# Float64 weights rounded inside four staging places, one per token block; the first layer's last output products moved into the second layer

## The chip, the core and the metric

The kernel runs on one core of a Trainium2 chip. The metric is device microseconds of one execution: the median of three runs before the change is 740.58 us (739.4 to 743.11). The profiled execution took 738.42 us, of which 736.6 us is the span from its first to its last instruction.

## The reference

`x` is (4, 8, 512, 64) and `state` (4, 8, 32, 64). A small attention step reads the state for each token and the tokens for each state row; its result, 2304 rows (4 x 512 tokens and 4 x 32 state rows) of 512, goes through two feed-forward layers:

```
h = x @ w_in;  g = max(h,0) + alpha*min(h,0);   x = g @ w_out      # layer 0: 512 -> 2048 -> 512
h = x @ w_in2; g = max(h,0) + log1p(exp(-|h|)); out = g @ w_out2   # layer 1: the same sizes
```

The weights arrive as float64. The kernel gets them as 64-bit integers and rounds them to float32 on the core.

## The kernel before, in words

**Precision.** Every float32 operand of a product is a pair (hi, lo): hi is a rounded copy, lo the rest, and a product is three matmuls, hi*hi, hi*lo, lo*hi (`mm3`, L180; `product`, L567). `split` (L185) makes a pair: a copy on ACT, a subtraction on DVE or POOL.

**Rounding one weight tile.** There are 64 tiles of 128x512, listed in `wsrc` (L193): 32 of layer 0 and 32 of layer 1, kinds `i` (w_in) and `o` (w_out). `wload` (L236) brings one tile's 64-bit words into one of three staging places `stg` (a fourth, borrowed from the accumulators, serves tile 3 alone). Five steps round it: `conv_a` on ACT (two passes, L264 and L265), `conv_j`, `conv_f`, `conv_v` on DVE (L269, L275, L279) and `conv_g` on POOL (L285). The result goes into one of three places `cnv`, taken round-robin by `cslot` (L257), except for layer 0's `i` tiles, which go to their own place. `wprep` (L296) then either splits the tile (layer 0, `o`) or stores it in DRAM (layer 1, L304). A staging place is free after `conv_v`, a `cnv` place after the split or the store has read it. `wo_load` (L481) brings stored `o` tiles back, also through `cnv`, and splits them from there.

**Layer 0** goes over four quarters q of the 2048 hidden columns. The attention step, quarter 0 and the first blocks of quarter 1 are in an order written out by hand (`ORDER`, L48). The rest is the loop at L911: per quarter 16 token blocks (b, fc) and one block of state rows (b = B). One block is `hidden` (6 matmuls), `act` (ACT `Relu` L398, DVE `prelu` L390, then `split` with both halves taken from PSUM) and `out_part` (12 matmuls, taken into the accumulators at L436 after each fourth block); `out_part` runs three blocks behind (`LAG`), from the list `todo`. `wconv` is called once per block, `wprep` as often as `READY` (L74) lists that block.

**Layer 1** is 16 groups (p, n). A group makes seven products (`product`, L571), additions of them on DVE (L474), four activations (three ACT passes L401 to L403, DVE L404, split) and the output products of the group before (`pair_out`, L580, taken in at L593). Its operands are cut and combined on ACT and POOL in `w_steps`, `y_first`, `y_second`. In the groups of p = 0, `wprep` is called three times per group (L987, L993, L1015) for the tiles that are left. Group (0, 0) begins by emptying `todo`: the three output products left from layer 0 (L962).

**Order.** Outside `ORDER` a planner places the instructions on the engines' queues by their order in the program and by its own estimate of when each is ready. On the chip each queue runs in order: an instruction that waits holds everything behind it. Loads, stores and reloads all leave from SP's queue. `psa` and `psb` have four PSUM banks each: `psa` for hidden values and layer 1's products, `psb` for output sums.

Of the kernel before, what the change touches and what calls it, by code (L numbers as in the profile page):

```python
# [8 lines left out]
F32 = mybir.dt.float32  # L9
# [9 lines left out]
P = 128  # L19
# [41 lines left out]
l13 I0 h14 v15 l14 D15 L18 g15 O14 J0 H16 w10 A16 C16 O15 p10 G16 q10 D16 H17 Q15 H18 A17 O16 C17 A18 G17
C18 D17 G18 D18 H19 h15 Q16 l15 H20 A19 C19 O17 A20 G19 C20 D19 G20 D20 w12 w13 p12 p13 q12 q13
# [23 lines left out]
def mixer_kernel(  # L86
# [98 lines left out]
    def split(eng_h, eng_l, h, l, src):  # L185
        if eng_h is nc.scalar:
            nc.scalar.activation(h, src, AF.Copy)  # L187
        else:
            eng_h.tensor_copy(h, src)
        eng_l.tensor_tensor(out=l, in0=src, in1=h, op=ALU.subtract)  # L190
# [8 lines left out]
    wsrc.insert(39, wsrc.pop(31))  # L199
# [7 lines left out]
    nload = [0]  # L207
    nconv = [0]
    nprep = [0]
# [25 lines left out]

    def wload():  # L236
        i = nload[0]
        if i < len(wsrc):
            to, of = stage(i).bitcast(U16), wsrc[i][4].bitcast(U16)
            nc.sync.dma_start(out=to[:, 0 : 4 * W - 1], in_=of[:, 1 : 4 * W])  # L240
            nload[0] += 1
# [13 lines left out]
    nc_ = [0]  # L255

    def cslot():  # L257
        nc_[0] += 1
        return cnv[(nc_[0] - 1) % len(cnv)]

# [26 lines left out]
    def wconv():  # L287
        i = nconv[0]
        if i >= len(wsrc) or i >= nprep[0] + len(cnv):
            return  # L290
        for step in (conv_a, conv_j, conv_f, conv_v, conv_g):
            step(i)
        wload()
        nconv[0] += 1

    def wprep(n=1):  # L296
        for _ in range(n):
            i = nprep[0]
            if i >= len(wsrc):
                return  # L300
            while nconv[0] < i + 1:
                wconv()
            if wsrc[i][1] == 1:
                nc.sync.dma_start(out=kept_w[wsrc[i][:4]], in_=rounded[i])  # L304
                stored.add(wsrc[i][:4])
            elif not is_whole(i):
                t = R(take_place(i))
                split(nc.scalar, nc.gpsimd, t[0], t[1], rounded[i])
            nprep[0] += 1


# [56 lines left out]
    def hidden(m, q, b, fc):  # L368

        if b < B:  # L370
            ps = bank(psa)
            f = slice(fc * P, (fc + 1) * P)
            ops = [(R(sw[b][k]), R(at[b][k])) for k in range(2)]
            for k, ((wh, wl), (xh, xl)) in enumerate(ops):
                mm3(ps, wh[:, f], wl[:, f], xh, xl, k == 0, k == len(ops) - 1)
            return ps
        ps = hidden_rows(m, q)
        hs = tslot()
        nc.scalar.activation(hs, ps, AF.Copy)
        ps = bank(psa)  # L380
# [13 lines left out]
    def act(m, q, b, fc, ps, to=None):  # L394
        gh, gl = R(to) if to else gslot()
        t = tslot()
        if m == 0:
            nc.scalar.activation(t, ps, AF.Relu, scale=-1.0)  # L398
            prelu(q, b, fc, t, ps)
        else:  # L400
            nc.scalar.activation(t, ps, AF.Abs)  # L401
            nc.scalar.activation(t, t, AF.Exp, scale=-1.0)  # L402
            nc.scalar.activation(t, t, AF.Ln, bias=1.0)  # L403
            nc.vector.scalar_tensor_tensor(out=ps, in0=ps, scalar=0.0, in1=t, op0=ALU.max, op1=ALU.add)  # L404
        split(nc.scalar, nc.vector, gh, gl, ps)
        return gh, gl
# [58 lines left out]
    g_free = [*g_p, wo_p[0], wo_p[1]]  # L465
# [15 lines left out]
    def wo_load(q, c):  # L481
        wprep(nconv[0] - nprep[0])
        assert ("o", 1, q, c) in stored
        t = cslot()
        nc.sync.dma_start(out=t, in_=kept_w["o", 1, q, c])
# [4 lines left out]
        split(nc.scalar, nc.gpsimd, *R(wo_ring[i]), t)  # L490
# [108 lines left out]
    def steps():  # L599
# [47 lines left out]
        @step  # L647
        def g(i):
            conv_g(i)
            nconv[0] += 1  # L650
            if is_whole(i):
                nprep[0] += 1
# [7 lines left out]
        def l(i):  # L660
            hi, lo = live["h", i]
            nc.gpsimd.tensor_tensor(out=lo, in0=rounded[i], in1=hi, op=ALU.subtract)
            nprep[0] += 1
# [247 lines left out]
    for q in range(1, NQ):  # L911
# [3 lines left out]
        for b in blocks:  # L915
            for fc in range(4 if b < B else 1):
                ps = hidden(0, q, b, fc)
# [4 lines left out]
                wconv()  # L922
# [4 lines left out]
                wprep(READY[q].count(n))  # L927
# [10 lines left out]

    before, wait_act = None, []
# [14 lines left out]
    for p in range(2):  # L954
        for n in range(8):
# [6 lines left out]
            if start:  # L962
                while todo:
                    out_part(*todo.pop(0))
# [13 lines left out]
            product(c, sums[2:], o, "t3", True)  # L978
            sub(nc.vector, u4, d, u2, ALU.add)
# [12 lines left out]
            if p == 0:  # L992
                wprep(n < 6)  # L993
# [20 lines left out]
            if p == 0:  # L1014
                wprep(n < 6)  # L1015
# [42 lines left out]
```

## Time and profile before

| | PE | DVE | ACT | POOL |
|---|---|---|---|---|
| busy us of 736.6 | 707.2 | 519.2 | 468.6 | 360.5 |
| share | 96% | 70% | 64% | 49% |

| | us |
|---|---|
| median of three runs | 740.58 |
| profiled execution | 738.42 |
| its span | 736.6 |
| PE idle in the span | 29.4 |

A share is an average over the attention step, layer 0 (to about 360 us) and layer 1. PE's idle time has to be looked up by stretch: the view by windows gives each engine's busy time, the granted TensorE clock (1.00 is 2.4 GHz, 0.50 is 1.2 GHz) and the DMA share of a stretch. In the view in order of time a row is: start us, duration us, engine, line, operation, out<-in, and in brackets the idle time before it and who released it.

### The profile page before, as it was taken

Reading aid. Unit: us, or ns where it says so; the run is one execution under the profiler, and the core shown is the slowest. Engines: PE = TensorE matmul, PEld = TensorE weight load, DVE = VectorE, ACT = ScalarE, POOL = GpSimd, SP = SyncE. Lnnn points to the kernel's source line nnn. Section 1 sums busy time; section 2 is a strip of 40 time slices with the busy share of each in tenths; the row PEclk is TensorE's granted clock in tenths of the full one; section 3 lists DMA queues with packets and bytes.
Section 4 is the critical chain, followed back from the end, with each engine's and each line's share of the span. In section 5 each row is a group of like instructions: output and inputs, shape, how many; then the busy total and the mean of one; then the engine's idle time right before and its main releaser. Section 6 shows DMA issues by size and latency. Waiting matters only on the chain.

```text
span 736.6 us, 10244 instructions
## 1 busy us (share of the span) xinstructions
PE 707.2 (96%) x3530; PEld 550.6 (75%) x3530; DVE 519.2 (70%) x840; ACT 468.6 (64%) x921; POOL 360.5 (49%) x401
## 2 busy tenths in 40 slices
PE   7899999999999899998979989999999999999997
PEld 5458777776777677866857868888888888888886
DVE  3999685699889847776563587856666646766665
ACT  4777695665665436565547886667685796676541
POOL 1553232253243202698836557865498765465110
PEclk9999999999999999999999999999999999999999
DMA  6542351143237503653040243311113321200003
GB/s 228 198 155 77 109 195 58 58 142 116 87 123 237 169 0 109 207 184 117 0 144 14 85 131 115 115 44 31 56 29 107 137 75 34 67 26 30 16 0 115
DMA packets 30484, 72.49 MB, mean 98 GB/s; under 512 B 3552, under 2 KB 3552, under 8 KB 30432
## 3 DMA queue, kind: packets, MB, share of 16 engines
q1 hardware_dynamic: 30432, 71.83, 30.5%
q8 instruction: 28, 0.46, 0.3%
q14 instruction: 24, 0.20, 0.1%
HBM read 58.97 MB, written 12.85 MB: 97 GB/s over the span
## 4 chain that ended last, share of the span: by engine, by line
PE 55%; POOL 5%; DMA 3%; ACT 1%; DVE 1%; issue 1%; DVEq 0%; POOLq 0%; SPq 0%; ACTq 0%
PE pa L571 19%; PE pb L181 10%; PE pb L182 10%; PE pb L183 10%; PE pa L181 2%; PE pa L182 1%; PE pa L183 1%; DMA wi<-cnv 1%; POOL cnv L285 1%; DMA at0l<-wi 1%; DMA stg<-w2i 1%; PE pa L326 1%; DMA wo<-cnv 1%; DVE cnv L279 1%; POOL at0l L474 0%
## 5 line engine op out<-in xcount | busy, mean ns | idle before, releaser
L285 POOL TENSOR_TENSOR cnv<-top,cnv 128x512 f32<-128x512 bf16 x48 | 59.2, 1233 | 67.9 <-DVE cnv L279 66.0
L593 DVE TENSOR_TENSOR acc<-pb,acc 128x512 f32<-128x512 f32 x112 | 74.7, 685 | 22.5 <-PE pb L183 21.6
L264 ACT ACTIVATE exp<-stg 128x512 bf16<-128x512 bf16 x63 | 42.2, 672 | 67.8 <-DVE cnv L279 27.6
L269 DVE SCALAR_TENSOR_TENSOR top<-stg,top 128x512 uint16<-128x512 uint16 x63 | 55.9, 889 | 27.4 <-ACT top L265 27.3
L401 ACT ACTIVATE tmp<-pa 128x512 f32<-128x512 f32 x68 | 40.0, 595 | 51.4 <-DVE pa L474 34.4
L390 DVE SCALAR_TENSOR_TENSOR pa<-tmp,rest,pa 128x512 f32<-128x512 f32 (+1 forms) x80 | 53.0, 666 | 23.4 <-ACT tmp L864 12.5
L404 DVE SCALAR_TENSOR_TENSOR pa<-pa,tmp 128x512 f32<-128x512 f32 x68 | 46.7, 693 | 19.4 <-ACT tmp L403 19.2
L279 DVE SCALAR_TENSOR_TENSOR cnv<-stg,exp 128x512 f32<-128x512 uint32 x48 | 43.5, 909 | 19.2 <-DMA wo<-cnv 6.5
L265 ACT ACTIVATE top<-exp,top_bias 128x512 uint16<-128x512 uint16 x64 | 46.0, 720 | 10.9 <-POOL cnv L285 6.8
L403 ACT ACTIVATE tmp<-tmp 128x512 f32<-128x512 f32 x68 | 42.4, 631 | 0.7
L402 ACT ACTIVATE tmp<-tmp 128x512 f32<-128x512 f32 x68 | 42.3, 632 | 0.6
L474 DVE TENSOR_TENSOR pa<-pa,wo2l 128x512 f32<-128x512 f32 x32 | 22.1, 695 | 22.5 <-PE pa L571 22.4
L436 DVE TENSOR_TENSOR acc<-pb,acc 128x512 f32<-128x512 f32 x54 | 35.3, 680 | 2.7 <-PE pb L183 2.7
L398 ACT ACTIVATE tmp<-pa 128x512 f32<-128x512 f32 x47 | 27.6, 589 | 12.1 <-PE pa L183 11.9
L190 POOL TENSOR_TENSOR wi4l<-at0h,wi4h 128x256 fp32r<-128x256 f32 x16 | 12.2, 768 | 34.9 <-ACT wi4h L187 33.5
L474 DVE TENSOR_TENSOR wo2h<-pa,wo2h 128x512 f32<-128x512 f32 x16 | 11.0, 690 | 25.4 <-ACT wo2h L967 13.3
L275 DVE TENSOR_SCALAR exp<-top 128x512 uint16<-128x512 uint16 x64 | 27.5, 432 | 0.5
L190 POOL TENSOR_TENSOR wo5l<-cnv,wo5h 128x512 fp32r<-128x512 f32 x9 | 11.7, 1301 | 30.2 <-ACT wo5h L187 30.1
L190 POOL TENSOR_TENSOR ex1l<-at1h,ex1h 128x256 fp32r<-128x256 f32 x16 | 12.3, 770 | 27.8 <-ACT ex1h L187 27.8
L187 ACT ACTIVATE g1h<-pa 128x512 fp32r<-128x512 f32 x26 | 15.5, 596 | 7.6 <-DVE pa L390 5.9
L190 DVE TENSOR_TENSOR g1l<-pa,g1h 128x512 fp32r<-128x512 f32 x26 | 17.8, 683 | 3.5 <-ACT g1h L187 3.3
L474 DVE TENSOR_TENSOR wo2l<-pa,wo2h 128x512 f32<-128x512 f32 x16 | 11.0, 689 | 12.6 <-PE pa L571 12.2
(801 smaller groups left out, 2470.5 us busy)
## 6 DMA issues: line engine op xcount, KB each, us to landing
cnv<-wo SPq DMA_DIRECT2D x32, 256.0 KB, 2.6
stg<-w1o SPq DMA_DIRECT2D x16, 511.8 KB, 3.4
stg<-w2i SPq DMA_DIRECT2D x16, 511.8 KB, 4.6
stg<-w2o SPq DMA_DIRECT2D x16, 511.8 KB, 3.5
stg<-w1i SPq DMA_DIRECT2D x15, 511.8 KB, 4.1
acc<-xt SPq DMA_DIRECT2D x16, 256.0 KB, 5.5
wi<-cnv SPq DMA_DIRECT2D x16, 256.0 KB, 3.9
wo<-cnv SPq DMA_DIRECT2D x16, 256.0 KB, 4.0
```

The lines of the kernel that those rows point to most:

```text
L181: nc.tensor.matmul(ps, lh, rh, start=start, stop=False)
L182: nc.tensor.matmul(ps, lh, rl, start=False, stop=False)
L183: nc.tensor.matmul(ps, ll, rh, start=False, stop=stop)
L190: eng_l.tensor_tensor(out=l, in0=src, in1=h, op=ALU.subtract)
L265: nc.scalar.activation(t.bitcast(U16), e.bitcast(U16), AF.Relu, bias=top_bias, scale=TOP_SCALE)
L269: nc.vector.scalar_tensor_tensor(out=tu, in0=words(i)[0], scalar=TOP_SIGN, in1=tu, op0=ALU.bitwise_and, op1=ALU.bitwise_or)
L279: nc.vector.scalar_tensor_tensor(out=a, in0=words(i)[1], scalar=REST, in1=parts(i)[1], op0=ALU.mult, op1=ALU.mult)
L285: nc.gpsimd.tensor_tensor(out=a, in0=parts(i)[0], in1=a, op=ALU.add)
L390: nc.vector.scalar_tensor_tensor(out=ps[:, cs], in0=t[:, cs], scalar=a, in1=ps[:, cs], op0=ALU.mult, op1=ALU.add)
L404: nc.vector.scalar_tensor_tensor(out=ps, in0=ps, scalar=0.0, in1=t, op0=ALU.max, op1=ALU.add)
L571: nc.tensor.matmul(ps, l[:, c], r, start=first and k == 0 and i == 0, stop=k == 1 and i == 2, skip_group_check=not first,)
L593: nc.vector.tensor_tensor(out=a, in0=ps, in1=a, op=ALU.add)
```

## The change

- The three `cnv` places go. A fourth staging place is added, and `conv_v` writes its result into the first half of the staging place that the tile was loaded to. The place is free only when the tile has been split or stored (or, for layer 0's `i` tiles, summed by `conv_g`), and only then may the load of the tile four further on be issued (`may_load`). In `ORDER` the loads L9, L16 and L17 stand later for that.
- `wconv`, `wprep` and `READY` are replaced by `conv_head` (the ACT passes, emitted before a block's `hidden`) and `tick` (the other steps, the split of the tile before, the loads now allowed, the store), once in each block named in `TICKS`, and by `GROUP_TICKS` in layer 1. `conv_head` is queued behind ACT's copy of the last activation, the DVE and POOL steps behind DVE's subtraction of it (`issue_after`, an order on the queue without a semaphore). 41 tiles are rounded in the loop over blocks, 7 in layer 1's groups 1 to 5.
- `wsrc` takes layer 1's first tiles earlier, so that two layer 0 tiles come when their places are free.
- `wo_load` brings a stored tile straight into the lo place of its pair, and splits it there.
- In a state-row block one `out_part` is put between ACT's copy of the rows and the PE transposes of it.
- The three output products left in `todo` are emitted at the start of group (0, 0), after its product `t3`, and at its end. `g_free` lists the places in the order in which they come free.

```diff
-READY = {1: (5, 6, ...), 2: (1, 2, 4, ...), 3: (0, 1, 2, 3, 4, 5)}
+TICKS = {1: range(4, 17), 2: range(17), 3: range(11)}
+GROUP_TICKS = (0, 2, 1, 1, 1, 2, 0, 0)
...
-    stg = [sbt([P, W], I64, f"stg{i}") for i in range(3)]
+    stg = [sbt([P, W], I64, f"stg{i}") for i in range(4)]
-    cnv = [sbt([P, W], F32, f"cnv{i}") for i in range(3)]
...
-    wsrc.insert(39, wsrc.pop(31))
+    first = wsrc[32:]
+    wsrc[32:] = []
+    late = [wsrc.pop(31), wsrc.pop(23)]
+    wsrc = wsrc[:23] + first[:5] + late[1:] + wsrc[23:] + first[5:14] + late[:1] + first[14:]
...
+    def may_load(i):
+        return i < 5 or (i - 4 if i > 7 else i - 5) in done_with
...
-        a = rounded[i] = take_place(i).f if is_whole(i) else cslot()
+        a = rounded[i] = take_place(i).f if is_whole(i) else stage(i).bitcast(F32)[:, 0:W]
...
-    def wconv():
-    def wprep(n=1):
...
+    def conv_head():
+        if nhead[0] == nconv[0] and nhead[0] < len(wsrc):
+            with tc.issue_after(acted["ACT"]) if acted else nullcontext():
+                conv_a(nhead[0])
+            nhead[0] += 1
+    def finish_splits():
+        while to_split:
+            i = to_split.pop(0)
+            t = R(take_place(i))
+            split(nc.scalar, nc.gpsimd, t[0], t[1], rounded[i])
+            done_with.add(i)
+    def tick():
+        i = nconv[0]
+        conv_head()
+        with tc.issue_after(acted["DVE"]):
+            for step in (conv_j, conv_f, conv_v, conv_g):
+                step(i)
+        nconv[0] += 1
+        finish_splits()
+        while nload[0] < len(wsrc) and may_load(nload[0]):
+            wload()
+        if wsrc[i][1] == 1:
+            nc.sync.dma_start(out=kept_w[wsrc[i][:4]], in_=rounded[i])
+            stored.add(wsrc[i][:4])
+            done_with.add(i)
+        elif is_whole(i):
+            done_with.add(i)
+        else:
+            to_split.append(i)
...
-        t = cslot()
-        nc.sync.dma_start(out=t, in_=kept_w["o", 1, q, c])
-        split(nc.scalar, nc.gpsimd, *R(wo_ring[i]), t)
+        hi, lo = R(wo_ring[i])
+        t = lo.bitcast(F32)
+        nc.sync.dma_start(out=t, in_=kept_w["o", 1, q, c])
+        split(nc.scalar, nc.gpsimd, hi, lo, t)
...
-                ps = hidden(0, q, b, fc)
+                if n in TICKS[q]:
+                    conv_head()
+                ps = hidden(0, q, b, fc) if b < B else turned_rows(rows_copy(0, q), lambda: out_part(*todo.pop(0)))
...
-                wconv()
+                if n in TICKS[q]:
+                    tick()
...
-                wprep(READY[q].count(n))
...
             if start:
-                while todo:
-                    out_part(*todo.pop(0))
+                out_part(*todo.pop(0))
...
             product(c, sums[2:], o, "t3", True)
+            if start:
+                out_part(*todo.pop(0))
...
-            if p == 0:
-                wprep(n < 6)
+            for _ in range(GROUP_TICKS[n] if p == 0 else 0):
+                tick()
+                conv_head()
...
+            if start:
+                out_part(*todo.pop(0))
```

## Rows read from the trace of the kernel before

**Rows 1.** Windows: PE, PEld, DVE, ACT, POOL busy (count), PEclk, DMA share, GB/s.
```profile
160.00:440.00 280.00, 262.52 (x1188) 201.18 (x1187) 203.47 (x320) 166.72 (x310) 138.73 (x140) 0.98 0.37 117
440.00:720.00 280.00, 280.00 (x1243) 231.88 (x1242) 184.17 (x285) 189.28 (x380) 165.84 (x211) 1.00 0.19 58
...
300.00:360.00 60.00, 55.19 (x231) 43.27 (x230) 42.35 (x64) 34.72 (x69) 53.54 (x55) 0.97 0.41 135
```

**Rows 2.** Order of time, PE, 230 to 430 us: the matmuls that PE waited for.
```profile
239.77 0.66 PE L382 MATMUL pa<-ident,tmp 128*128 128x128 f32 x4 [0.69 <-ACT tmp L379]
...
252.00 1.03 PE L326 MATMUL pa<-wi3h,ex0h 64*32 64x512 f32 x2 [1.97 <-DVE g2l L190]
...
323.27 0.66 PE L382 MATMUL pa<-ident,tmp 128*128 128x128 f32 x4 [1.15 <-ACT tmp L379]
...
337.30 0.66 PE L181 MATMUL pb<-wo5h,g3h 128*128 128x512 f32 x1 [3.61 <-ACT exp L264]
...
382.00 0.80 PE L571 MATMUL pa<-at7h,ex1h 128*128 128x512 f32 x1 [2.89 <-DVE pa L474]
...
387.23 0.50 PE L181 MATMUL pb<-wo3h,g0h 128*128 128x512 f32 x1 [2.31 <-ACT g0h L187]
...
427.78 0.50 PE L181 MATMUL pb<-wo6h,g2h 128*128 128x512 f32 x1 [2.44 <-ACT g2h L187]
```

**Rows 3.** Windows just behind three of these waits.
```profile
252.00:254.00 2.00, 2.00 (x13) 0.33 (x13) 1.98 (x4) 0.47 (x1) 0.00 (x0) 0.52 0.87 316
...
337.40:342.40 5.00, 5.00 (x15) 3.92 (x16) 5.00 (x8) 3.23 (x6) 5.00 (x5) 0.66 0.56 187
...
387.30:392.30 5.00, 5.00 (x15) 3.97 (x16) 3.82 (x6) 3.80 (x8) 0.28 (x1) 0.66 0.19 52
```

**Rows 4.** Order of time, ACT, ahead of the wait at 252 us.
```profile
244.45 0.66 ACT L264 ACTIVATE exp<-stg 128x512 bf16<-128x512 bf16 x1 [2.25 <-DMA stg<-w2i]
245.20 0.72 ACT L265 ACTIVATE top<-exp,top_bias 128x512 uint16<-128x512 uint16 x1
246.85 0.66 ACT L264 ACTIVATE exp<-stg 128x512 bf16<-128x512 bf16 x1 [0.93 <-DMA stg<-w2i]
247.41 0.59 ACT L398 ACTIVATE tmp<-pa 128x512 f32<-128x512 f32 x1
```

**Rows 5.** Order of time, SP and DVE, ahead of the wait at 337 us.
```profile
333.22 0.32 SPq L304 DMA_DIRECT2D wi<-cnv  x1
...
335.86 0.69 DVE L279 SCALAR_TENSOR_TENSOR cnv<-stg,exp 128x512 f32<-128x512 uint32 x1 [0.86 <-DMA wi<-cnv]
```

**Rows 6.** Order of time, DVE and ACT, ahead of the waits at 382 and 428 us.
```profile
380.64 0.69 DVE L279 SCALAR_TENSOR_TENSOR cnv<-stg,exp 128x512 f32<-128x512 uint32 x1 [3.58 <-DMA wo<-cnv]
381.37 0.67 ACT L264 ACTIVATE exp<-stg 128x512 bf16<-128x512 bf16 x1 [6.69 <-DVE cnv L279]
...
424.60 0.69 DVE L279 SCALAR_TENSOR_TENSOR cnv<-stg,exp 128x512 f32<-128x512 uint32 x1 [2.13 <-DMA wi<-cnv]
```

**Rows 7.** Single lines, the DVE steps of the rounding: duration ns min/median/max.
```profile
L269 DVE SCALAR_TENSOR_TENSOR top<-stg,top x63: 674/693/1724, 11.2 to 460.6; 128x512 uint16<-128x512 uint16 x63
...
L275 DVE TENSOR_SCALAR exp<-top x64: 230/286/1379, 12.6 to 462.3; 128x512 uint16<-128x512 uint16 x64
...
L279 DVE SCALAR_TENSOR_TENSOR cnv<-stg,exp x48: 628/693/2400, 32.8 to 471.3; 128x512 f32<-128x512 uint32 x48
```

**Rows 8.** Groups by line: count | busy us, mean ns | idle before, releasers.
```profile
L285 POOL TENSOR_TENSOR cnv<-top,cnv 128x512 f32<-128x512 bf16 x48 | 59.2, 1233 | 67.9 <-DVE cnv L279 66.0 <-PE pb L183 1.2 <-PE pa L571 0.6
...
L390 DVE SCALAR_TENSOR_TENSOR pa<-tmp,rest,pa 128x512 f32<-128x512 f32 x64 | 47.7, 746 | 17.3 <-ACT tmp L398 9.5 <-ACT tmp L864 7.7
...
L436 DVE TENSOR_TENSOR acc<-pb,acc 128x512 f32<-128x512 f32 x54 | 35.3, 680 | 2.7 <-PE pb L183 2.7
```

**Rows 9.** DMA issues: count, KB each, median us from issue to landing.
```profile
stg<-w2i SPq DMA_DIRECT2D x16, 511.8 KB, 4.6
...
wi<-cnv SPq DMA_DIRECT2D x16, 256.0 KB, 3.9
```

More of the change, by code (lines that the diff above doesn't have):

```diff
@@ L1 @@
-from contextlib import ExitStack
+from contextlib import ExitStack, nullcontext
 import concourse.bass as bass
@@ new lines @@
+b0 j2 g1 x3 B0 y0 L4 m1 L5 c0 f2 a3 d0 u1 v2 e1 N29 S2 j3 L6 g2 z1 k2 k3 N3 R0 f3 n1 Z0 t2 v3 F0 a4 b1 N4 X0
+g3 t3 x4 W0 m2 N8 w00 a5 w01 j4 p00 m3 f4 e2 N2 H0 u3 p01 z2 e3 H1 v4 n2 c1 z3 L7 A0 y1 g4 C0 b2 A1 q01 n3 c2
+h4 G0 d1 C1 w03 a6 D0 d2 l4 H2 p03 j6 G1 O0 j5 A2 D1 C2 f6 G2 f5 v6 H3 D2 g6 v5 h6 b3 L8 g5 A3 y2 x5 q03 c3 l6
+h5 C3 w02 a7 M1 d3 M2 G3 p02 l5 L9 H4 D3 a8 j7 H5 q02 A4 E2 O1 f7 E1 j8 A5 v7 f8 L10 g7 x6 C5 v8 S4 a9 Z1 g8
+C4 O2 Z2 h7 G4 l7 j9 G5 k4 k5 O3 a10 D4 D5 f9 t4 v9 H6 Q3 m4 g9 t5 H7 M4 u4 A6 m5 E4 O4 C6 e4 u5 G6 z4 e5 A7
@@ L63 @@
+h12 D14 W6 l12 L16 f14 a15 X7 w11 W7 O13 j15 p11 v14 f15 h13 g14 q11 G15 l13 L17 I0 h14 v15 l14 D15 L18 g15
+O14 J0 H16 w10 A16 C16 O15 p10 G16 q10 D16 H17 Q15 H18 A17 O16 C17 A18 G17 C18 D17 G18 D18 H19 h15 Q16 l15 H20
+A19 C19 O17 A20 G19 C20 D19 G20 D20 w12 w13 p12 p13 q12 q13
 """.split()
@@ L185, in split @@
     def split(eng_h, eng_l, h, l, src):
[L186 to L190, printed above, removed]
+        a = nc.scalar.activation(h, src, AF.Copy) if eng_h is nc.scalar else eng_h.tensor_copy(h, src)
+        return a.ins, eng_l.tensor_tensor(out=l, in0=src, in1=h, op=ALU.subtract).ins
     wsrc = []
@@ L207, in mixer_kernel @@
     nload = [0]
+    nhead = [0]
     nconv = [0]
-    nprep = [0]
+    to_split = []
+    done_with = set()
     def weight(*key):
@@ L238, in wload @@
         if i < len(wsrc):
+            assert may_load(i)
             to, of = stage(i).bitcast(U16), wsrc[i][4].bitcast(U16)
@@ L254, in mixer_kernel @@
     stored = set()
[L255 to L259, printed above, removed]
     def conv_a(i):
@@ L285, in conv_g @@
         nc.gpsimd.tensor_tensor(out=a, in0=parts(i)[0], in1=a, op=ALU.add)
-    def wconv():
-        i = nconv[0]
[L289 to L293, printed above, removed]
-        nconv[0] += 1
-    def wprep(n=1):
[L297 to L301, printed above, removed]
-                wconv()
[L303 to L309, printed above, removed]
+    acted = {}
+    def conv_head():
[10 more added lines that the diff above has]
+    def tick():
+        i = nconv[0]
+        conv_head()
+        with tc.issue_after(acted["DVE"]):
+            for step in (conv_j, conv_f, conv_v, conv_g):
+                step(i)
+        nconv[0] += 1
+        finish_splits()
[9 more added lines that the diff above has]
+            to_split.append(i)
     def col(g, k, hh):
@@ L376, in hidden, with rows_copy @@
             return ps
+        return turned_rows(rows_copy(m, q))
+    def rows_copy(m, q):
         ps = hidden_rows(m, q)
@@ L379, in hidden, with turned_rows @@
         nc.scalar.activation(hs, ps, AF.Copy)
+        return hs
+    def turned_rows(hs, between=None):
+        if between:
+            between()
         ps = bank(psa)
@@ L404, in act @@
             nc.vector.scalar_tensor_tensor(out=ps, in0=ps, scalar=0.0, in1=t, op0=ALU.max, op1=ALU.add)
-        split(nc.scalar, nc.vector, gh, gl, ps)
+        acted["ACT"], acted["DVE"] = split(nc.scalar, nc.vector, gh, gl, ps)
         return gh, gl
@@ L464, in mixer_kernel @@
     nwo = [0]
-    g_free = [*g_p, wo_p[0], wo_p[1]]
+    g_free = []
     def wo_of(q, c):
@@ L650, in g @@
             nconv[0] += 1
+            nhead[0] += 1
             if is_whole(i):
-                nprep[0] += 1
+                done_with.add(i)
         @step
@@ L662, in l @@
             nc.gpsimd.tensor_tensor(out=lo, in0=rounded[i], in1=hi, op=ALU.subtract)
-            nprep[0] += 1
+            done_with.add(i)
         def scores(*groups):
@@ L937, in mixer_kernel @@
                 n += 1
+    g_free += [g_p[(ng[0] + i) % 4] for i in range(3)] + [wo_p[0], g_p[(ng[0] + 3) % 4], wo_p[1]]
     before, wait_act = None, []
```

31 lines of the change are left out of this document (6 added, 25 removed).

## The prediction

> **What bounds the kernel now.** I read the windows first, coarse ones, because a share over the span mixes stages. From 440 to 720 us PE is busy for all of 280 us at the full granted clock [rows 1]: layer 1's groups past the second quarter have nothing to give, whatever happens on the other engines. 1243 matmuls in 280 us are 0.225 us each; this is my price for a 512-column matmul below. From 160 to 440 us, layer 0's loop and the first groups, PE is busy 262.5 of 280 us and the clock is 0.98 of full [rows 1]. So 17.5 us of waiting and about 0.02 x 280 = 5.6 us of slow clock lie there: 23.1 us in all, and that is the ceiling of any gain from better order. What lies before 160 us is the written order, which the change hardly touches.
>
> Second, the order of time of PE alone: the brackets give each wait. Seven of them hold 0.69 + 1.97 + 1.15 + 3.61 + 2.89 + 2.31 + 2.44 = 15.1 of the 17.5 us [rows 2]. Third, the windows behind the longer ones: 0.52 for 2 us, 0.66 for 5 us, 0.66 for 5 us [rows 3]. The clock falls towards its lower level after PE has stood, and each such stretch costs work: 0.48 x 2 = 1.0, 0.34 x 5 = 1.7 and 1.7 us. 1.2 us of slow clock is spread over the rest.
>
> Fourth, the queues of the other engines ahead of each wait, since PE's releaser is only the last link. At 252 us PE waits for a subtraction on DVE; ACT, which feeds it, had stood 2.25 and 0.93 us in the first rounding pass for a weight load, with the block's own activation (L398) behind it [rows 4]. At 337 us the first link is a store: it is issued at 333.22 us, DVE's last rounding step waits for it until 335.86, because it writes the `cnv` place which the store reads [rows 5], and the next rounding pass on ACT, which PE's row names, is behind that. At 382 and 428 us it is the same: DVE stands 3.58 and 2.13 us for a store, and ACT 6.69 us behind it [rows 6]. At 240 and 323 us PE waits for ACT's copy of a row block before its transposes [rows 2]. So nearly every wait is a rounding step that waits for a transfer at the head of an engine's queue.
>
> **The change part by part**, against the profiled execution, 738.4 us (span 736.6 and 1.8 around it).
>
> *No `cnv` places.* The last DVE step no longer waits for a store, as it writes where its own tile lies. The wait at 337 us goes: 3.61 + 1.7 of clock = 5.3 us. The wait at 428 us goes: 2.4 us.
>
> *One tile per block, behind the activation.* The bursts go, and with them the wait at 252 us: 1.97 + 1.0 = 2.9 us. What is spread over short waits (17.5 - 15.1 = 2.4 us, and 1.2 us of clock) comes from the same crowding; I take half, 1.8 us.
>
> *Row blocks.* An `out_part`, 12 x 0.225 = 2.7 us of PE work, lies over an ACT copy of about 0.6 us (as L398 in [rows 4]): 0.69 + 1.15 = 1.8 us go.
>
> *The last output products later, no rounding in group 0.* DVE's stop at 380 us is gone, so the additions that PE wants at 382 run about 3.6 us sooner, and ACT starts its activations before 381 instead of after. Two output products, 5.4 us of PE work, now lie where PE found nothing. 2.89 + 2.31 + 1.7 = 6.9 us; I keep 1.0 us back, because a first activation is still three ACT passes, a DVE pass and a copy, some 3 us.
>
> Gains: 5.3 + 2.4 + 2.9 + 1.8 + 1.8 + 5.9 = 20.1 us.
>
> *What it adds.* (a) A place is now held from load to store. A tile's round is: load 4.6, store 3.9 [rows 9], two ACT passes 0.66 + 0.72, `Relu` 0.59 [rows 4], `prelu` 0.75, ACT's copy 0.59, subtraction 0.68 (as the pass at L436), POOL sum 1.23 [rows 8], and the three DVE steps 0.69 + 0.29 + 0.69 = 1.67 at their medians [rows 7]: 15.4 us. Four blocks are 4 x 18 x 0.225 = 16.2 us before row blocks. It fits with 0.8 us to spare. With the DVE steps at their longest, 1.72 + 1.38 + 2.40 = 5.5 [rows 7], the round is 19.2 us, 3.0 too long, and behind it wait ACT's next `Relu` and SP's next stores. 41 tiles are some 10 rounds: 0 to 31 us. I take 1.0, near the lower end, since the medians are far from the longest and three blocks of `LAG` absorb a late one.
> (b) DVE: a block is 0.75 + 0.68 + 0.68 = 2.1 us and the rounding 1.67, 3.8 of PE's 4.05 us. If each step took half a POOL pass more, 1.67 + 3 x 0.6 = 3.5 and 5.6 us, 1.5 over, on 30 blocks up to 46 us; but POOL has just one sum per block there, which starts when the DVE steps are over. 0 to 46; I take 1.5, near the medians.
> (c) Last quarter: POOL is busy 53.5 of 60 us, DVE 42.4 [rows 1]. Five blocks (n = 6 to 10) round while the cuts run. At the longest steps this is 5 x (5.5 - 1.67) = 19 us of DVE, of which its 17.6 idle us hide nearly all: 0 to 19, I take 2.0.
> (d) L9 waits for a split now. Bounds 0 and one landing, 4.6 us [rows 9]; an `out_part` and two `hidden` (24 matmuls, 5.4 us) lie between it and its use: 0.5.
> (e) `wo_load` into the lo place waits until PE has read that place; load 3.9 (as the store in [rows 9]), copy 0.6, POOL pass 1.23 = 5.7 us follow. Its user is a group later, and a group is 42 + 48 matmuls, 20 us: nothing. Without that cover 5.7 us for each of 14 groups. SP's loads behind it have the same room.
>
> The Trainium skill ("SBUF — State Buffer", section "SBUF: two separate sides") speaks against (c): DVE and GpSimd share one port pair, which the instruction that starts first holds until it ends. By it every rounding step that meets a POOL pass waits for its end, and in the last quarter, where POOL nearly always runs, the sum would have most of the 19 us of (c) instead of 2.0. The spread of L269, 693 ns at the median and 1724 at most [rows 7], agrees with a wait of one POOL pass, but the median says that most steps don't meet one.
>
> Costs: 1.0 + 1.5 + 2.0 + 0.5 = 5.0. Net 20.1 - 5.0 = 15.1 us: 738.4 - 15.1 = 723.3 us of an execution like the profiled one. The median of the runs lies 2.2 us above the profiled execution; I add a third of it: 724 us.
>
> **The rivals.**
> 1. *DVE and POOL set layer 0's pace.* (b) and (c) eat the gains of layer 0's loop (2.9 + 5.3 + 1.8), and what is left is the row blocks and layer 1: 1.8 + 5.9 + 2.4 = 10.1. For it: 3.8 of 4.05 us, and POOL at 89%. Against it: DVE's 203 of 280 us, bursts included [rows 1]. 740.6 - 10 = 730.5 us.
> 2. *The staging round is too long*: slower. If load and store take 1 us more each and a step meets one POOL pass, the round is 15.4 + 2 + 1.2 = 18.6 us, 2.4 over; each `conv_a` then stands at the head of ACT's queue for its load, with `Relu` behind it, in 10 rounds: 24 us, and the loop's gains are lost. 740.6 - 10.1 + 24 = 754 us. It decides where a round passes 16.2 us, and costs more than the change gains from about 17.2 on. For it: ACT already stands for loads [rows 4], with more buffers. Against: it needs most tiles late, not the odd one.
> 3. *The waits only move*: a rounding pass waits for its load instead of a store, as long and as often, and PE's waits come back a block later. The order behind the activation is one of queues and takes no wait away. 740 us.
> 4. *All of it comes*: all waits go and (a) to (d) are hidden. 740.6 - 23 = 717 us.
>
> **How the numbers follow.** Forecast 0.57 (its own range 719 to 729), rival 1 0.17, rival 2 0.09, rival 3 0.10, rival 4 0.07. A measurement of this kernel tells 0.5%, 3.7 us, from no change. Faster by more: forecast, rivals 1 and 4, 0.81. Within: rival 3, 0.10. Slower: rival 2, 0.09. The range leaves out rivals 2 and 3 and takes in the others with their edges: 716 to 736 us; its upper end is the forecast with 12 us more of (a) to (c).
>
> **What would show it.** Right: PE has no wait over 1 us between 330 and 400 us that begins at a DVE rounding step; the windows after 160 us show a clock of 1.00; rounding steps come once per block, with L279 near 0.69 us; the span is some 15 us shorter, all of it before layer 1's second quarter, and the 280 us of full PE reappear. Wrong: ACT's first rounding pass waits for loads by tens of us in total (rival 2), DVE is over 95% busy in quarters 1 and 2 (rival 1), or PE's waits in quarter 2 grow. A row of PE idle behind `wo_load`'s splits would refute (e).

## The result, and the profile after

The changed kernel takes 718.18 us (median of 4 runs, 716.8 to 718.72), against 740.98 us of the kernel before in the same session: ratio 0.9688, 95% interval 0.9659 to 0.9717, or 22.8 us less. The forecast was 724 us in 716 to 736. The profiled execution of after took 718.6 us, span 716.8.

The windows of after, with the columns of [rows 1]; the gain shifts layer 1 by 20 us, so 420 to 700 answers to 440 to 720.

```profile
160.00:420.00 260.00, 254.43 (x1184) 199.19 (x1184) 205.17 (x320) 168.58 (x313) 140.41 (x142) 0.99 0.39 125
420.00:700.00 280.00, 280.00 (x1242) 231.86 (x1242) 182.61 (x289) 190.96 (x382) 165.35 (x211) 1.00 0.18 59
300.00:340.00 40.00, 34.43 (x133) 25.84 (x133) 34.67 (x48) 21.19 (x41) 37.13 (x39) 0.91 0.50 165
300.00:325.00 25.00, 22.71 (x92) 16.33 (x91) 20.48 (x29) 14.35 (x30) 25.00 (x30) 1.00 0.44 149
328.40:333.40 5.00, 5.00 (x12) 3.95 (x13) 5.00 (x8) 3.00 (x5) 4.17 (x4) 0.50 0.65 249
```

The 1184 matmuls that answer to the 1188 of before take 260 us instead of 280, and the full stretch of layer 1 is as it was. All that PE still waits for from 160 us on lies in 300 to 340 us: it is busy 34.43 of 40 us, with POOL busy for all of 300 to 325.

PE in order of time: the rows that answer to [rows 2] at 239.77, 323.27, 337.30 and 427.78 us, and the one other wait over 0.3 us.

```profile
234.95 0.60 PE L395 MATMUL pa<-ident,tmp 128*128 128x128 f32 x4
...
307.64 0.47 PE L177 MATMUL pb<-g3h,wo5h 128*128 128x512 f32 x1 [1.04 <-DVE acc L449]
...
313.83 0.66 PE L395 MATMUL pa<-ident,tmp 128*128 128x128 f32 x4
...
328.28 0.77 PE L177 MATMUL pb<-wo5h,g3h 128*128 128x512 f32 x1 [4.48 <-DVE acc L449]
...
408.26 0.39 PE L177 MATMUL pb<-wo6h,g2h 128*128 128x512 f32 x1
```

Subtracting starts gives the gain by place: 4.8 us by the first, 9.4 by the third, 9.0 by the fourth, 19.5 by the last, 19.8 at the span's end. So the loop up to the last quarter's row block gave 9.4 us, the last quarter gave nothing (the wait of 3.61 us at 337 became one of 4.48 at the same product, with the clock at 0.50 for 5 us behind it), and the groups of layer 1 gave 10.5.

ACT in order of time where [rows 4] had rounding passes that waited for loads:

```profile
238.88 0.59 ACT L182 ACTIVATE g2h<-pa 128x512 fp32r<-128x512 f32 x1
239.35 0.66 ACT L260 ACTIVATE exp<-stg 128x512 bf16<-128x512 bf16 x1
240.11 0.73 ACT L261 ACTIVATE top<-exp,top_bias 128x512 uint16<-128x512 uint16 x1
241.04 0.60 ACT L411 ACTIVATE tmp<-pa 128x512 f32<-128x512 f32 x1 [0.20 <-PE pa L179]
```

The first rounding pass (L260) stands right behind an activation's copy (L182 into `g2h`) and waits for nothing; the next `Relu` waits for PE, not for a load.

### The profile page after: what moved, and what is told of

Its sections match the earlier page's. It is cut to its first block, busy times and chain, and to the rows that moved or that the text cites. A ratio compares the mean times of both kernels' runs of the same rounds, so it can differ in the third digit from the quotient of the medians.

```text
span 716.8 us, 10219 instructions
## 1 busy us (share of the span) xinstructions
PE 702.4 (98%) x3530; PEld 550.5 (77%) x3530; DVE 511.5 (71%) x840; ACT 469.3 (65%) x921; POOL 359.1 (50%) x401
## 4 chain that ended last, share of the span: by engine, by line
PE 82%; DVE 11%; DMA 2%; issue 2%; ACT 1%; POOL 1%; SPq 0%; DVEq 0%; ACTq 0%
PE pa L584 21%; PE pb L177 15%; PE pb L178 15%; PE pb L179 15%; PE pa L177 3%; PE pa L179 3%; PE pa L178 3%; DVE top L265 2%; DVE pa L403 1%; PE pa L367 1%; DVE acc L449 1%; PE pa L331 1%; DVE stg L275 1%; DMA acc<-xt 1%; DVE exp L271 1%
## 5 line engine op out<-in xcount | busy, mean ns | idle before, releaser
L281 POOL TENSOR_TENSOR stg<-top,stg 128x512 f32<-128x512 bf16 x48 | 57.7, 1203 | 107.0 <-DVE stg L275 71.3
L403 DVE SCALAR_TENSOR_TENSOR pa<-tmp,rest,pa 128x512 f32<-128x512 f32 (+1 forms) x80 | 52.9, 668 | 28.7 <-ACT tmp L411 14.5
L265 DVE SCALAR_TENSOR_TENSOR top<-stg,top 128x512 uint16<-128x512 uint16 x63 | 53.0, 846 | 16.1 <-ACT top L261 15.7
L260 ACT ACTIVATE exp<-stg 128x512 bf16<-128x512 bf16 x63 | 42.1, 671 | 22.4 <-DMA stg<-w1i 7.3
L275 DVE SCALAR_TENSOR_TENSOR stg<-stg,exp 128x512 f32<-128x512 uint32 x48 | 39.5, 825 | 0.9
L487 DVE TENSOR_TENSOR pa<-pa,wo2l 128x512 f32<-128x512 f32 x32 | 22.3, 697 | 23.0 <-PE pa L584 22.8
L449 DVE TENSOR_TENSOR acc<-pb,acc 128x512 f32<-128x512 f32 x54 | 35.1, 682 | 3.6 <-PE pb L179 3.6
L411 ACT ACTIVATE tmp<-pa 128x512 f32<-128x512 f32 x47 | 27.2, 588 | 13.5 <-PE pa L179 8.3
L182 ACT ACTIVATE g1h<-pa 128x512 fp32r<-128x512 f32 x26 | 15.5, 596 | 17.3 <-DVE pa L403 9.4
L271 DVE TENSOR_SCALAR exp<-top 128x512 uint16<-128x512 uint16 x64 | 25.0, 394 | 0.7
L183 POOL TENSOR_TENSOR ex1l<-at1h,ex1h 128x256 fp32r<-128x256 f32 x16 | 12.3, 774 | 26.0 <-ACT ex1h L182 24.0
L182 ACT ACTIVATE g0h<-pa 128x512 fp32r<-128x512 f32 x23 | 13.7, 596 | 13.1 <-DVE pa L403 11.1
L183 DVE TENSOR_TENSOR g3l<-pa,g3h 128x512 fp32r<-128x512 f32 x22 | 15.1, 687 | 9.9 <-ACT g3h L182 9.9
L183 POOL TENSOR_TENSOR wo5l<-wo5l,wo5h 128x512 fp32r<-128x512 f32 x8 | 10.4, 1298 | 22.9 <-ACT wo5h L182 22.6
```

Of the source, the lines that this page charges most:

```text
L265: nc.vector.scalar_tensor_tensor(out=tu, in0=words(i)[0], scalar=TOP_SIGN, in1=tu, op0=ALU.bitwise_and, op1=ALU.bitwise_or)
L275: nc.vector.scalar_tensor_tensor(out=a, in0=words(i)[1], scalar=REST, in1=parts(i)[1], op0=ALU.mult, op1=ALU.mult)
L281: nc.gpsimd.tensor_tensor(out=a, in0=parts(i)[0], in1=a, op=ALU.add)
L403: nc.vector.scalar_tensor_tensor(out=ps[:, cs], in0=t[:, cs], scalar=a, in1=ps[:, cs], op0=ALU.mult, op1=ALU.add)
L487: eng.tensor_tensor(out=o, in0=x, in1=y, op=op)
```

## The experiments

Ratios are to runs of the kernel before in the same session. No kernel leaves out a part of the computation. There are three suspects: the places (no `cnv`, rounding in place), the pace (one tile per block) and the queue order (`issue_after`).

**Pace alone, on the kernel before.**

```diff
-READY = {1: (5, 6, ...), 2: (1, 2, 4, ...), 3: (0, 1, 2, 3, 4, 5)}
+READY = {1: range(4, 17), 2: range(17), 3: range(11)}
+GROUP_TICKS = (0, 2, 1, 1, 1, 2, 0, 0)
...
-    wsrc.insert(39, wsrc.pop(31))
+    first = wsrc[32:]
...
```

> The kernel before, its three staging and three cnv places kept, but with the weights taken in the new order and one tile rounded per token block (41 in the loop, 7 in layer 1's groups 1 to 5). Theory (pace and places both count: the bursts made the waits up to 290 us, the cnv places made those at 337, 382 and 428 us by a DVE step that waits for a store): the span up to the second quarter's last block gets some 9 us shorter as in the changed kernel, the waits at DVE for stores stay, about 729 us. Rival (the pace alone does it): 718 to 721 us, with DVE waiting for stores under 3 us in total. Rival (only the places count): 738 to 741 us.

743.35 us, ratio 1.0055 (1.003 to 1.008): slightly slower, and above all three ranges. DVE waits for no store of a `cnv` place any more from 160 to 440 us (before: 4.8 + 3.0 us), and yet the window has no gain (before: 262.52, clock 0.98):

```profile
160.00:440.00 280.00, 259.50 (x1162) 198.01 (x1161) 208.36 (x324) 165.14 (x303) 150.46 (x142) 0.96 0.37 125
```

**Places and pace without the order**: the kernel after with both `issue_after` taken out.

```diff
-            with tc.issue_after(acted["ACT"]) if acted else nullcontext():
+            with nullcontext():
                 conv_a(nhead[0])
...
-        with tc.issue_after(acted["DVE"]):
+        with nullcontext():
             for step in (conv_j, conv_f, conv_v, conv_g):
```

> The changed kernel without the order behind the activation: the planner places the rounding steps where it likes. Theory (pace and places do it; the order on the queues only settles ties): 718 to 721 us. Rival (the order is what keeps a late load from standing ahead of an activation): 724 us or more, with PE waits of 1 to 2 us in quarters 1 and 2 whose releasers lead back to ACT's first rounding pass waiting for a load.

739.66 us, ratio 1.001 (0.9995 to 1.0025). Four places, an even pace, no `cnv`, the row-block edit and the moved output products together bring nothing once the order is gone. Two views show what came back. ACT's waits from 160 to 440 us, by what ended them (us in total, times, longest):

```profile
ACT exp L260 <- DMA stg<-w2i: 21.4, 9, 4.7
ACT exp L260 <- DVE stg L275: 13.7, 8, 2.9
...
ACT exp L260 <- DMA stg<-w2o: 6.7, 3, 3.3
ACT exp L260 <- DMA stg<-w1i: 5.4, 4, 2.9
```

and one wait in order of time, from ACT over DVE to PE:

```profile
280.92 0.65 ACT L260 ACTIVATE exp<-stg 128x512 bf16<-128x512 bf16 x1 [4.69 <-DMA stg<-w2i]
...
282.30 0.58 ACT L411 ACTIVATE tmp<-pa 128x512 f32<-128x512 f32 x1
...
282.42 0.69 DVE L265 SCALAR_TENSOR_TENSOR top<-stg,top 128x512 uint16<-128x512 uint16 x1 [5.09 <-ACT top L261]
...
284.08 0.75 DVE L403 SCALAR_TENSOR_TENSOR pa<-tmp,rest,pa 128x512 f32<-128x512 f32 x1
286.08 0.69 DVE L183 TENSOR_TENSOR g0l<-pa,g0h 128x512 fp32r<-128x512 f32 x1 [1.25 <-ACT g0h L182]
...
286.83 0.53 PE L177 MATMUL pa<-at6h,sw6h 128*128 128x512 f32 x1 [2.35 <-DVE g0l L183]
```

A rounding pass stands 4.69 us on ACT for its load, the block's `Relu` (L411) behind it; DVE stands 5.09 us for that rounding pass, and `prelu` (L403) and the subtraction (L183) that PE waits for come behind it.

The same view of waits in after:

```profile
ACT exp L260 <- DMA stg<-w2i: 6.1, 4, 2.3
...
ACT exp L260 <- DVE stg L275: 3.8, 5, 2.0
...
ACT exp L260 <- DMA stg<-w1o: 1.6, 1, 1.6
ACT exp L260 <- DMA stg<-w2o: 0.8, 1, 0.8
```

and in the kernel before:

```profile
ACT exp L264 <- DVE cnv L279: 22.7, 12, 6.7
...
ACT exp L264 <- DMA stg<-w2i: 12.3, 9, 2.9
```

Placed freely, rounding passes stand on ACT's queue before their loads have landed, with activations behind them: the rows of first passes that wait for loads sum to 33.5 us here and to 8.5 in after. By the same sums the kernel before has 18.8 us, before_paced 24.7 (it lost its store waits and got more load waits), and the two kernels below that keep the order and the old places 6.6 and 1.8. The waits of the same pass for DVE's last rounding step fall too, from 13.7 us here to 3.8 in after; no run separates what each of the two costs PE.

**Order and pace, with the places of before**: three `stg`, three `cnv`, the old place of the last output products, no row-block edit.

```diff
+        acted["ACT"], acted["DVE"] = split(nc.scalar, nc.vector, gh, gl, ps)
...
-        for step in (conv_a, conv_j, conv_f, conv_v, conv_g):
-            step(i)
+        conv_head()
+        with tc.issue_after(acted["DVE"]):
+            for step in (conv_j, conv_f, conv_v, conv_g):
+                step(i)
```

> The kernel before with its three staging and three cnv places, one tile per block as in before_paced, and now with the order behind the activation on ACT's and DVE's queues. New theory (the order is the change: it keeps the rounding from running ahead of its loads; the places matter little): ratio 0.970 to 0.980, the waits at 200, 262 and 396 us of before_paced gone. Old theory (the places made most of the gain): 0.985 or more, with DVE waiting for stores as before.

718.52 us, ratio 0.9693 (0.9664 to 0.9723), just under its theory's range: the time of after, without three of its parts. No wait of DVE for a store of a `cnv` place is left from 160 to 440 us, though the places are there. PE's two waits over 1 us:

```profile
325.95 0.47 PE L178 MATMUL pb<-wo5h,g3h 128*128 128x512 f32 x1 [3.15 <-DVE acc L442]
371.19 0.80 PE L178 MATMUL pa<-wi4h,srh 128*128 128x512 f32 x1 [2.04 <-DVE g1l L184]
```

After has 4.48 instead of 3.15 us at the first product and no wait at the second. So the three parts are not shown to be worth nothing each: what they bring and cost offsets here.

**The order alone**: the kernel before with its bursts, and `conv_a` behind ACT's copy, the other steps behind DVE's subtraction.

```diff
-        for step in (conv_a, conv_j, conv_f, conv_v, conv_g):
-            step(i)
+        with tc.issue_after(acted["ACT"]):
+            conv_a(i)
+        with tc.issue_after(acted["DVE"]):
+            for step in (conv_j, conv_f, conv_v, conv_g):
+                step(i)
```

> The kernel before with nothing of the change but the queue order: the ACT passes of the rounding behind the last activation's copy, the other steps behind DVE's subtraction of it. The three stg and three cnv places, the bursts of READY, the old list of tiles and the old places of the last output products all stay. Theory (the order is what moves the time): most of the gain comes, as the steps can no longer be put ahead of the activations, and the bursts of splits cost little: 720 to 727 us, ratio 0.975 to 0.985. Rival (order needs the even pace: with bursts, stores and splits come together, the cnv places stay full and the order only holds steps back): 733 to 742 us, ratio 0.99 to 1.00, with waits of DVE's last rounding step for a store still over 2 us.

730.91 us, ratio 0.9881 (0.9851 to 0.9911): outside both ranges. The windows split it by stage (before: PE 135.05 and 127.47 of 140):

```profile
160.00:300.00 140.00, 139.99 (x697) 107.02 (x696) 113.89 (x186) 81.36 (x146) 45.38 (x40) 1.00 0.35 115
300.00:440.00 140.00, 126.94 (x536) 100.85 (x535) 98.34 (x141) 89.78 (x178) 99.14 (x103) 0.96 0.36 113
```

Up to 300 us the order alone is enough, bursts and `cnv` places included. From 300 on nothing is gained. There ACT waits for a reload through `cnv`, and PE stands 7.53 us (ACT, then PE, in order of time):

```profile
374.98 0.63 ACT L186 ACTIVATE wo6h<-cnv 128x512 fp32r<-128x512 f32 x1 [10.56 <-DMA cnv<-wo]
...
380.71 0.80 PE L181 MATMUL pa<-wi4h,srh 128*128 128x512 f32 x1 [7.53 <-DVE g1l L187]
```

That reload was issued only at 372.17 us. With the new pace and list, which leave no rounding in group 0, cnv_ordered has 2.04 us at the same product. So order and pace need each other: the pace alone gives 1.0055, the order alone 0.9881, both 0.9693.

**Each half of the order.** Two kernels like after: ACT's `issue_after` alone, and DVE's alone (the other one a `nullcontext()`).

> The changed kernel with the order behind the activation on ACT alone; the DVE and POOL steps go where the planner likes. New theory (what harms is an ACT rounding pass that waits for its load with an activation behind it): ratio 0.967 to 0.975. Rival (DVE's three passes, let free, are put ahead of a block's own passes and cost as much): 0.985 or more.

> The kernel after with the queue order on the DVE and POOL steps alone; the ACT passes are placed freely. ACT's half alone gave 722.66 us (0.9755), both 718.2 (0.969), neither 739.66 (1.001). Theory (what costs is an ACT pass that stands at the head of ACT's queue for its load, ahead of an activation; the DVE half only adds): 730 to 738 us, ratio 0.986 to 0.998, with PE waits of 2 to 4 us as without any order. Rival (either half is enough, since the ACT passes of the next tile can't run far ahead of the DVE steps with two top places): 719 to 725 us, ratio 0.971 to 0.979.

ACT's half gives 722.66 us, 0.9755 (0.9726 to 0.9784), DVE's half 726.41 us, 0.9818 (0.9791 to 0.9844); each lies between the two ranges written for it, ACT's only just. From 160 to 300 us PE is busy 137.45 and 135.11 of 140 us, with both 140.00. Each half carries much of the gain. A possible reason, which no run tests, is that the steps of one tile are a chain, so that holding back one end holds back part of the other.

**The staging round.** The load of a tile is allowed only when the tile three before is done, from tile 20 on: it is emitted one tile later in the program.

```diff
-        return i < 5 or (i - 4 if i > 7 else i - 5) in done_with
+        return i < 5 or (i - (3 if i > 19 else 4) if i > 7 else i - 5) in done_with
```

> The changed kernel with each load in the loop allowed one tile later, as if there were three staging places: a load may leave only when the tile three before it is done. Theory of the staging round (15.4 us from load to store; three blocks are 12.2 to 13.4 us): ACT stands for its load in most rounds, 2 to 3 us a round in 41/3 = 14 rounds, so 28 to 42 us if nothing hides it, ratio 1.00 to 1.02. Rival (the round is much shorter than its sum, for stores land in 2.6 us and not 3.9): 0.967 to 0.975.

717.52 us, ratio 0.9689 (0.9666 to 0.9712); 160 to 300 us has PE at 140.00. But this does not test the round. The same load in SP's rows, in after and then in loads_later:

```profile
235.20 0.33 SPq L242 DMA_DIRECT2D stg<-w2i  x1
```

```profile
235.03 0.33 SPq L242 DMA_DIRECT2D stg<-w2i  x1
```

The loads leave in the same order and, from 200 to 340 us, within 1.0 us of the same times, where one block later would be some 4 us. The edit moved them in the program and not on the chip, so how near rival 2 is stays open. That it does not hold with four places is seen in after itself: 8.5 us of waits for loads and a full PE up to 300 us.

**The last output products** all at the start of group (0, 0), as before.

```diff
-                out_part(*todo.pop(0))
+                while todo:
+                    out_part(*todo.pop(0))
...
-            if start:
-                out_part(*todo.pop(0))
...
-            if start:
-                out_part(*todo.pop(0))
```

> The changed kernel with the three last output products all at the start of layer 1's first group, as before. Theory (DVE's stop for a store at 380 us was most of that place's loss, the products were merely moved): PE finds a wait of 1 to 3 us between its products and its first output products of layer 1, with a slow clock behind it: 720 to 723 us. Rival (the moved products are what filled the 9.6 us gained there): 725 us or more. Rival (they do nothing, since rounding left the first group): 718 us.

721.37 us, 0.9768 (0.9736 to 0.9799), in the theory's range. That is 3 us more than after by the medians of two sessions, 6 by the ratios; the profile accounts for some 2 of them. The wait that is new to it has the length of the one in cnv_ordered, the other kernel with the old place, and the clock behind it stays at 1.00:

```profile
373.67 0.50 PE L177 MATMUL pa<-wi4h,srh 128*128 128x512 f32 x1 [2.04 <-DVE g1l L183]
```

**A lighter last quarter.** Five tiles of quarter 3 go to layer 1's groups.

```diff
-TICKS = {1: range(4, 17), 2: range(17), 3: range(11)}
-GROUP_TICKS = (0, 2, 1, 1, 1, 2, 0, 0)
+TICKS = {1: range(4, 17), 2: range(17), 3: range(6)}
+GROUP_TICKS = (0, 3, 2, 2, 2, 3, 0, 0)
```

> The changed kernel with the last five tiles of the last quarter (blocks 6 to 10, where the cuts run on POOL) rounded in layer 1's groups instead: 12 tiles there, three in groups 1 and 5, two in 2 to 4. Theory (POOL, full from 300 to 325 us, makes the one long PE wait left, 4.5 us at 328 us with slow clock behind it): that wait goes or halves, 712 to 715 us, and layer 1 keeps a full PE. Rival (the wait comes from the cuts alone, or the groups pay for the five tiles): 717 to 722 us.

711.75 us, ratio 0.9633 (0.961 to 0.9657), the fastest version. Its windows:

```profile
160.00:440.00 280.00, 279.19 (x1310) 220.39 (x1309) 216.43 (x347) 183.69 (x345) 153.51 (x161) 1.00 0.35 115
...
300.00:340.00 40.00, 39.19 (x169) 30.47 (x168) 24.32 (x38) 21.59 (x41) 38.78 (x43) 1.00 0.30 99
```

In 300 to 340 us POOL is still nearly full (38.78), but DVE falls from 34.67 to 24.32 us and PE's 4.48 us wait is gone. So a full POOL alone does not make PE wait.

**What holds the last quarter.** In after, POOL, ACT and DVE in order of time ahead of that wait:

```profile
320.43 1.42 POOL L183 TENSOR_TENSOR ex0l<-at0l,ex0h 128x256 fp32r<-128x256 f32 x2
321.82 1.17 POOL L281 TENSOR_TENSOR stg<-top,stg 128x512 f32<-128x512 bf16 x1
...
323.02 0.72 ACT L261 ACTIVATE top<-exp,top_bias 128x512 uint16<-128x512 uint16 x1 [2.28 <-POOL stg L281]
323.65 0.58 ACT L182 ACTIVATE g0h<-pa 128x512 fp32r<-128x512 f32 x1
...
325.47 1.86 DVE L265 SCALAR_TENSOR_TENSOR top<-stg,top 128x512 uint16<-128x512 uint16 x2
...
327.45 0.68 DVE L449 TENSOR_TENSOR acc<-pb,acc 128x512 f32<-128x512 f32 x1
```

ACT stands at the second rounding pass until POOL's sum (L281), which comes behind the cuts, has read `top`; the copy of an activation is behind it. On DVE two rounding steps then come ahead of the addition (L449) that PE's row names. So a third `top` and a third `exp` place:

```diff
-    top_t = [[sbt([P, W], BF16, f"{x}{i}") for i in range(2)] for x in ("top", "exp")]
+    top_t = [[sbt([P, W], BF16, f"{x}{i}") for i in range(3)] for x in ("top", "exp")]
```

> The kernel after with three top and three exp places instead of two, nothing else. In the last quarter of the kernel after an ACT pass of the rounding waits 2.28 us for POOL's sum of an earlier tile, which reads top, and PE waits 4.48 us a little later. Theory (POOL is full there and late, and through the two top places it holds ACT and so the activations): the wait of PE between 300 and 340 us falls under 2 us, 714 to 716 us, ratio 0.964 to 0.967. Rival (POOL's own work in that quarter, the cuts that come between, sets the pace with or without a third place): 717.5 to 719.5 us, ratio 0.969 to 0.971, with the wait of some 4 us still there.

722.14 us, 0.9764 (0.9734 to 0.9793): slower than after, and in neither text's range. In order of time, ACT and then PE:

```profile
317.46 0.67 ACT L260 ACTIVATE exp<-stg 128x512 bf16<-128x512 bf16 x1 [1.42 <-DMA stg<-w2o]
318.02 0.59 ACT L387 ACTIVATE tmp<-pa 128x512 f32<-128x512 f32 x1
...
318.66 1.11 PE L395 MATMUL pa<-ident,tmp 128*128 128x128 f32 x4 [3.48 <-ACT tmp L387]
```

The 4.48 us wait went and one of 3.48 us came: part of it, 1.42 us, is a rounding pass that now waits for its load, ahead of the row copy. The first passes' waits for loads in 160 to 440 us rise from 8.5 to 18.5 us. That the two places alone hold the quarter is not borne out; what the runs show is that the quarter gains when rounding leaves it.

**The best version with the old places**: cnv_ordered with the output products moved and the lighter last quarter, but still without the row-block edit.

> Three stg and three cnv places as in the kernel before (no rounding in place, no split straight from the lo place), but with one tile per block, the queue order, the last output products moved, and five tiles of the last quarter given to layer 1's groups. Theory (the places are worth nothing; order, output products and the lighter last quarter are all of it): 709 to 715 us, ratio 0.960 to 0.967, like the fastest version so far with four places (711.75 us, 0.9633). Rival (the places are needed once the rest is right, as a store then holds DVE in the groups of layer 1): 717 to 722 us, ratio 0.97 to 0.976.

716.17 us, ratio 0.9681 (0.9653 to 0.9708), between both texts. It is some 4 us or 0.5% slower than ticks_to_groups, with intervals that just touch. The places and the row-block edit share this. The profile points to a row block (PE) and to the reloads (ACT, then PE):

```profile
314.74 0.66 PE L388 MATMUL pa<-ident,tmp 128*128 128x128 f32 x4 [1.14 <-ACT tmp L385]
...
404.94 0.63 ACT L183 ACTIVATE wo4h<-cnv 128x512 fp32r<-128x512 f32 x1 [3.15 <-DMA cnv<-wo]
...
408.51 0.80 PE L178 MATMUL pa<-wi4h,srh 128*128 128x512 f32 x1 [2.61 <-DVE g1l L184]
```

**The kernel after once more**, beside four of these.

> The changed kernel itself, once more, beside the runs to come on the same chip, since their bounds lie close together. Every theory: ratio 0.966 to 0.972.

718.41 us, ratio 0.9699 (0.9668 to 0.973), with the same wait of 4.49 us in the last quarter.

## Why the prediction was right, and where it was wrong

The sign came out and the time lies in the stated range; the cause of most of it did not. 718.18 us lies just below the forecast's own 719 to 729 and nearest to rival 4's 717, which had 0.07, but rival 4's condition, that all waits go, does not hold: 5.6 us of waiting are left in 300 to 340 us. Against the forecast's 15.1 us, by stretch of the profiled executions:

| stretch (start of its last row in [rows 2]) | forecast | measured |
|---|---|---|
| to 323.27: 2.9 + 1.8 + 1.8, less (a), (b), (d) 3.0 | 3.5 | 9.4 |
| to 337.30: 5.3, less (c) 2.0 | 3.3 | -0.4 |
| to 427.78: 5.9 + 2.4 | 8.3 | 10.5 |
| to the end | 0 | 0.3 |

- *No `cnv` places: 5.3 + 2.4.* Wrong as a cause. The 5.3 us at 337 did not come: PE waits 4.48 us for the same product with no store in the chain [rows 5]. The store was the last link of a late ACT and DVE, not their reason: DVE was idle for it for only 0.86 us [rows 5], and ahead of that ACT's second rounding pass had stood 3.00 us for POOL's sum, as it does in after (2.28 us, ahead of 323.02). The row stands below. before_paced, where DVE waits for no store, is no faster. In cnv_ordered the same places stay and the time is that of after. The 2.4 us at 428 came, and cnv_ordered, with the old places, has no wait there either.
- *One tile per block: 2.9 + 1.8.* The half that I named first, the bursts, is worth nothing by itself (1.0055). The order is what takes the loop's waits away: with it PE is full up to 300 us even with bursts (order_alone). What was "spread over short waits" was mostly two waits, 1.41 us at 169.79 and 0.89 at 188.17, and their last link is no transfer: rounding steps stood on DVE among the block's own passes. At the second, a step of 1.23 us ran ahead of a subtraction whose input, ACT's copy, was there at 186.40 (rows below). This is also where rival 3 was argued wrongly: "takes no wait away". A wait at a queue's head costs by what stands behind it, and the order changes that. Rival 3's outcome, waits that only move and 740 us, is what free_order shows: the change without its order.
- *Row blocks: 1.8.* Both waits are gone, but the edit can claim little of it. At 239.77 the kernels with the order and without the edit (cnv_ordered, order_alone, cnv_best) have no wait over 0.3 us. At 323.27 they have 0.55, 2.06 and 1.14 us; free_order, act_order_only and top3, with the edit, have 2.24, 2.25 and 3.48. No run takes the edit alone.
- *Group 0: 5.9.* All of it came. The moved products are worth about 2 us of it by the profile (outs_at_start, a 2.04 us wait with no slow clock behind it). That the rest goes with rounding that no longer stands in group 0 is argued from 7.53 us in order_alone against 2.04 in cnv_ordered, which differ in the whole pace and list. The 1.0 us that I kept back was not spent.
- *(a) the staging round: 1.0.* Nothing that shows: PE is full up to 300 us. How much room is left in the round no run shows (loads_later did not move the loads).
- *(b) DVE's pace: 1.5.* Nothing, though DVE's steps are longer than their medians: in 160 to 300 us a tile takes 25.12/31 + 12.05/30 + 23.31/30 = 1.99 us on L265, L271 and L275 instead of 1.67 (2.07 by the same sum in before), and PE is full with DVE at 125.32 of 140 us.
- *(c) the last quarter: 2.0.* Too low. It is the one place where after is no faster, and moving five tiles out of it gives 4 us more by the ratios (0.9688 to 0.9633), 6.4 by the medians of two sessions (718.18 to 711.75). Rival 1's mechanism is real there and only there. The rule of the Trainium skill ("SBUF — State Buffer", section "SBUF: two separate sides") is borne out in part only: where POOL is busy 37.13 of 40 us the steps of a tile take 8.06/7 + 4.58/7 + 7.76/7 = 2.91 us, 0.92 more than in the loop. That is far from the 5.5 us of the longest steps, and in 340 to 440 us, with POOL at 65.41 of 100, four tiles take 1.87 us each. Seven tiles lose 6.4 us of DVE, and which share of it reaches PE no run separates.
- *(d), (e): 0.5 and 0.* Nothing: after 50 us the two waits shown are the only ones of PE over 0.3 us in after, and neither is behind L9 or a reload.

The rows of the kernel before that the first two points name (ACT at 328; DVE and PE at 188):

```profile
328.25 0.72 ACT L265 ACTIVATE top<-exp,top_bias 128x512 uint16<-128x512 uint16 x1 [3.00 <-POOL cnv L285]
...
186.29 1.23 DVE L269 SCALAR_TENSOR_TENSOR top<-stg,top 128x512 uint16<-128x512 uint16 x1
187.44 0.68 DVE L190 TENSOR_TENSOR g1l<-pa,g1h 128x512 fp32r<-128x512 f32 x1
...
188.17 0.50 PE L181 MATMUL pa<-at6h,sw6h 128*128 128x512 f32 x1 [0.89 <-DVE g1l L190]
```

So the sum was near because two errors met, which is luck: the loop's gain was sized too low (short waits and slow clock came back whole, not half, which makes 8.3 of the 9.4 us, and the costs were not there; 1.1 us stay open), and a gain was booked in the last quarter that did not come. The ceiling of 23.1 us was wrong too: the span of ticks_to_groups is 26.6 us shorter than before's. Beside 17.5 us of waiting, PE's busy time had more to give than the 5.6 us priced by a clock of 0.98: 262.52 us for 1188 matmuls in before, 252.19 us for 1189 in 160 to 413 us of ticks_to_groups. What stays open: each version is planned anew, so differences of some 3 us (the moved products, the places in the best version) may hold a share of other placements, as top3's 4 us in the wrong direction shows. The same holds for differences of that size between sessions.

## What to carry to other kernels

Where a planner fills in-order queues, look for instructions that stand at a head waiting for a transfer with critical work behind them, and tie them behind that work before adding buffers: here the order was worth 3.2% on top of the even pace (1.001 to 0.969) and 1.2% on the bursts, and four places and the pace without it nothing. The releaser that a row names is the last link; whether it is the cause shows only when it is taken away alone. When a stretch is filled, look for the stretch that gained nothing, since load moved out of it (here five tiles, 0.6%) is the next gain.

## What the runs showed of the hardware

- The rounding steps on DVE took 1.99 us a tile with POOL at 50.78 of 140 us and 2.91 with 37.13 of 40, but 1.87 with 65.41 of 100 (all in after): POOL's share alone does not set their length.
- The store of a layer 1 tile takes 2.6 and 2.5 us from issue to landing in after (`i` and `o` tiles) and 2.3 and 2.0 in free_order, both from a staging place; from a `cnv` place it takes 3.9 and 4.0 before [rows 9], and 3.1 and 4.0 in cnv_ordered with the even pace. So it goes more with the places than with the spacing; why, no run separates. The loads did not become faster: 4.6, 3.4, 4.1 and 3.5 us before for the tiles of w2i, w1o, w1i and w2o, and 4.2, 4.3, 4.5 and 3.4 in after.
- PE waits of 1.04 us (after), 1.14 (cnv_best) and 1.41 (before) were followed by 5 us at a granted clock of 1.00. The wait of some 4.5 us in the last quarter was followed by 5 us at 0.50, the lower level of 1.2 GHz, in after, but at 0.66 and 0.70 in after_again and outs_at_start. Waits of 2.04 us were followed by 0.67 in cnv_ordered and by 1.00 in outs_at_start: the length of a wait alone does not tell what follows it.
